# Expert 1's rows turned by TensorE from copies instead of through memory, and a new order around the late tiles

## The chip, the cores and the metric

The kernel runs on one core of a Trainium2 chip. Its time is the device time of one execution in microseconds (us); lower is better. TensorE (PE in the profile) multiplies, VectorE (DVE), ScalarE (ACT) and GpSimd (POOL) do the elementwise work, and SyncE (SP) issues most of the DMAs.

## The reference

Retention over 8 batches, 8 heads, 576 positions and head dimension 64, and then a mixture of experts on its output (4608 tokens of width 512, 8 experts of hidden width 1024):

```python
scores = (q @ k.T) / 8                       # per batch and head
ret = scores * gamma[h] ** (i - j)           # where j <= i, else 0
x = (ret @ v), heads side by side            # 4608 x 512
do = x @ w_skip > 0                          # tokens below stay as they are
e = argmax(x[do] @ w_gate); g = softmax(x[do] @ w_gate)[e]
y = g * (relu(x[do] @ w1[e]) @ w2[e])        # one expert for each token
out = x;  out[do] += y
```

## The kernel before, in words

**Retention.** The 4608 tokens are 36 tiles of 128; a batch is 4.5 tiles, so two batches make nine tiles, and `place(g)` is a tile's number among them. Each tile loads `q_t[g]` (queries and keys, turned) and `v_t[g]` (values, and keys as rows for the running state), 512 KB each, by `load` on SyncE's queue; six tiles of the first and four of the second are in flight. TensorE forms scores, state, values and the part carried from the state; VectorE applies masks and decays (`causal`, `decayed`); GpSimd scales the values (`scale`). `stage_c` turns the tile back, and it is written to `out`. The state ends with the tile whose place is 8: `state` returns there at once.

**Routing.** Logits come by four tiles. `GROUPS` are runs of tiles after which `route` picks each token's expert, its gate and its rank among its expert's tokens. It is a generator, and `spare` lets it run in VectorE's spare time of each tile. Its `gates` ends in five small operations by `pool` on GpSimd, which write the gate in three parts and the products `mc`. `slot_match` and `slot_add` then give the slots of tokens as a matrix product into `ps_m`. After the second group the most frequent expert so far is chosen to be expert 0 (`choose_first`), and its weights are loaded while retention still runs: chunk f at tick `LOADED[f]`, its high half cast on ScalarE two ticks later, its low half made on GpSimd in pieces by `lower`. After the fourth group (`KCUT`, tiles 24 to 27) `close_first` fetches the first 256 rows of expert 0, and GpSimd copies them by chunk (`by_chunk`) for `turn_early` on TensorE.

**Experts.** Weights come in 64 chunks (expert, eighth of the hidden width) of 512 KB into four raw tiles (`RAW`) and are split in a high and a low half (`split_w`: ScalarE the high, VectorE the low); each product is three matmuls. Expert 0 has up to 368 rows, in three blocks. The two early blocks run through chunks 0 to 5 as soon as they are there: `up_early`, `rectify`, `down_early`. The third block, `late`, is fetched by `late_ids` when all tiles are routed, turned by `turn_first`, and runs through these chunks by `up_late` and `down` in `experts`, six steps with the product of step f behind the up of step f + 1. In a late step ScalarE copies `part` out of PSUM, and VectorE makes `part`, `hhil` and `hlol` of it (lines 544 to 548). From chunk 6 on all three blocks run together, and then the other experts, one chunk after the other; `between` holds work to be done at places (expert, chunk, 0 before the down or 1 behind it).

**The next expert's rows** are gathered by indirect DMAs (`gather_next`), stored to memory (`stow`), read back by quarters of their columns (`spread`), turned in 32x32 blocks on VectorE (`turn_quarters`) and split in halves (`split_turned`). For expert 1 the store is issued on SyncE ahead of the weights of expert 1, the read at the end of step 5.

**Small work around it.** `expert_ids` writes the order of the experts, of which SyncE loads registers for the addresses of weights. `slot_rest` makes the target rows and gates that `finish` needs, `rank_caps` the room of each expert, which only `count_more` reads at the end.

**What sets the order.** TensorE's instructions stand in the order written. So do all that `vec`, `pool` and `keep` issue, on their engines. ScalarE's copies and casts are free: a scheduler places them by its own estimate of when they are ready. Each engine then runs its queue in order.

Of the kernel before, what the change touches and what calls it, by code (L numbers as in the profile page):

```python
# [23 lines left out]
P = 128  # L24
# [6 lines left out]
Q = 32  # L31
# [20 lines left out]
RAW = 4  # L52
GROUPS = (8, 8, 8, 4, 8)
KONE = 1
LOADED = (0, 3, 6, 8, 10, 12)
KCUT = 3
LAST = len(GROUPS) - 1
CUT = 2 * P
# [7 lines left out]
def kernel(  # L66
# [132 lines left out]
    def route(ps, k, post):  # L199

        t0, n = starts[k], GROUPS[k]
        nb = [P, n, NE]
        l8 = lg[:, t0 : t0 + n, 0:NE]
        mx = rt.tile([P, n], F32, tag="mx", name=f"mx_{t0}")
        vec("tensor_reduce", mx, l8, axis=AX.X, op=ALU.max)
        yield 210
        ls = rt.tile(nb, F32, tag="ls", name=f"ls_{t0}")
        vec("tensor_tensor", ls, l8, mx.unsqueeze(2).broadcast_to(nb), ALU.subtract)
        yield 210
        ex = rt.tile(nb, F32, tag="ex", name=f"ex_{t0}")  # L210
        nc.scalar.activation(ex, ls, AF.Exp)
        oh = rt.tile(nb, F32, tag="oh", name=f"oh_{t0}")
        vec("scalar_tensor_tensor", oh, ls, 0.0, desc.unsqueeze(1).broadcast_to(nb), ALU.is_equal, ALU.mult)
        yield 210
        m2 = rt.tile([P, n], F32, tag="m2", name=f"m2_{t0}")
        vec("tensor_reduce", m2, oh, axis=AX.X, op=ALU.max)
        yield 210
        vec("tensor_tensor", oh, oh, m2.unsqueeze(2).broadcast_to(nb), ALU.is_equal)
        yield 210
        mb = mks[:, t0 : t0 + n, :]  # L220
        skip = lg[:, t0 : t0 + n, NE : NE + 1].broadcast_to(nb)
        vec("scalar_tensor_tensor", mb, skip, 0.0, oh, ALU.is_gt, ALU.mult)
        yield 210
        at = flushed[0]
        pe.append(lambda: ranks(ps, k, mb))
        if k < LAST:
            yield from total(k, mb)
            if k == KONE:
                pe.append(lambda: count(ps, cum[:, k + 1, :], CNT))
        yield from gates(t0, n, ex, mb)  # L230
        while flushed[0] == at:
            yield WAIT
        mk = rt.tile(nb, F32, tag="mk", name=f"mk_{t0}")
        c0 = NE * NCMP * NBLK + t0 * NE
        vec("tensor_tensor", mk, ps[:, c0 : c0 + n * NE].rearrange("p (t e) -> p t e", e=NE), mb, ALU.mult)
        yield 210
        vec("tensor_reduce", trank[:, t0 : t0 + n], mk, axis=AX.X, op=ALU.add)
        yield 210
        if k == KONE:
            yield from choose_first(ps)  # L240
        for t in range(t0, t0 + n):
            while len(rs_t) == NR:
                yield WAIT
            slot_match(t)
            adds.append(lambda t=t: slot_add(ps, t, False, t == NT - 1))
            yield 260
        if post:
            at = flushed[0]
            pe.append(lambda: count(ps, cum[:, k + 1, :], CNT + NE))
            while flushed[0] == at:  # L250
                yield WAIT
            yield from post()
# [25 lines left out]
        vec("tensor_tensor", cum[:, k + 1, :], cum[:, k, :], some, ALU.add)  # L278
        yield 200

    def gates(t0, n, ex, mb):
        sm = rt.tile([P, n], F32, tag="sm", name=f"sm_{t0}")
        vec("tensor_reduce", sm, ex, axis=AX.X, op=ALU.add)
        yield 210
        vec("tensor_scalar", sm, sm, 1e-9, None, ALU.add)
        yield 200
        gt = rt.tile([P, n], F32, tag="gt", name=f"gt_{t0}")
        vec("reciprocal", gt, sm)
        yield 200
        cp = comps[:, t0 : t0 + n, :]  # L290
        pool("tensor_copy", cp[:, :, 2], gt)
        pool("tensor_tensor", gt, gt, cp[:, :, 2], ALU.subtract)
        pool("tensor_copy", cp[:, :, 3], gt)
        pool("tensor_tensor", cp[:, :, 4], gt, cp[:, :, 3], ALU.subtract)
        pool(
            "tensor_tensor",
            mc[:, t0 : t0 + n, :].rearrange("p t (e k) -> p t e k", k=NCMP),
            mb.unsqueeze(3).broadcast_to([P, n, NE, NCMP]),
            cp.unsqueeze(2).broadcast_to([P, n, NE, NCMP]),
            ALU.mult,  # L300
        )
# [252 lines left out]
    with ExitStack() as actx:  # L554
# [8 lines left out]

        q_t, v_t = {}, {}

        def behind(ins, other):
            tc.add_manual_dep(
                ins.ins,
# [4 lines left out]

        def load(into, n, g):
            into[g] = ap.tile([P, 2, DM], F32, tag="qv"[n], name=f"{'qv'[n]}_{g}", bufs=(QBUFS, VBUFS)[n])
            nc.sync.dma_start(into[g].rearrange("p s i -> p (s i)"), qkv[g, n])

        load(q_t, 0, 0)
        nc.scalar.dma_start(tt_sb, ttab)
# [41 lines left out]

        def head(a, r):
            return 2 * a + (r ^ (a & 1))

        def place(g):
            return g % NPD

        def scores(g):

# [442 lines left out]
    def spread(e):  # L1072

        n = span(e)
        xq[e] = mp.tile([P, -(-CAPS[1] // Q), P], F32, tag="xq", name=f"xq_{e}", bufs=1)
        for q in range(NQD):
            rows = xr[e][:, q * P : (q + 1) * P].rearrange("(g a) f -> a g f", a=Q)
            keep(nc.sync.dma_start(xq[e][q * Q : (q + 1) * Q, : n // Q, :], rows))

    def turn_quarters(e, c):  # L1080

# [13 lines left out]
    def experts():  # L1095
# [20 lines left out]
        def at(e, f, place, do, *args):  # L1116
            between.setdefault((e, f, place), []).append(lambda: do(*args))

        def turn_next(e):
            xT[e] = [mp.tile([P, NCC, CAP], F32R, tag=x, name=f"{x}_{e}") for x in ("xhi", "xlo")]  # L1120
            if e > 1:
                at(e - 1, 0, 1, lambda: stow(e, xg[e]))
                at(e - 1, 2, 0, spread, e)
            places = [(4, 0), (5, 0), (5, 1), (6, 0), (7, 0)] if e > 1 else [(6, 0), (6, 1), (7, 0), (7, 1), (7, 1)]
            for c, where in enumerate(places):
                if c:
                    at(e - 1, *where, split_turned, e, *xT[e], c - 1)
                if c < NCC:
# [1 line left out]

        at(NE - 1, 4, 1, count_more)
        for e in range(2, NE):
            at(e - 2, 4, 1, lambda e=e: gather_next(e, xg))

        load_raw(NFC - 1)
        gather_next(1, xg)
        by_chunk(*late[0], nc.scalar.copy)
        down_early(4)
        turn_first(late, range(NCC), "pt")
        down_early(5)  # L1140
        expert_ids()
        regs[1:] = expert_regs()[1:]
        split_raw(1)
        slot_rest(idf)
        rank_caps()
        stow(1, xg[1])
        py[0].append(bank("py2", "py_0_2"))
        turn_next(1)
        at(0, NCUT - 1, 1, spread, 1)
        for cur in steps + [None]:  # L1150
            if cur:
                e, f, ks = cur
# [29 lines left out]
            for do in between.pop((*place, 1), ()) if place else ():  # L1182
                do()
            if cur:
                split_raw(sum(chunks.index(c) < i + AHEAD for c in raw))
                load_raw(len(chunks))
            last = cur
        assert not between

    py = {0: [bank(f"py{c}", f"py_0_{c}") for c in range(CUT // P)]}  # L1190

    def down_early(f):
        down(0, f, early, py[0], hs[0, f], wq[0, f])

    for f in range(2, NCUT):
        hs[0, f] = hidden(mp, f)
    down_early(0)
    rectify(phs[2], early, hs[0, 2])
    rectify(phs[3], early, hs[0, 3])
    flush()  # L1200
    late_ids(ps_m)
    rectify(phs[4], early, hs[0, 4])
    down_early(1)
# [5 lines left out]
    count(ps_m, cum[:, LAST + 1, :], CNT + 2 * NE)  # L1209
    up_early(5)  # L1210
    rank_experts(ps_m)
    rectify(phs[5], early, hs[0, 5])
    idf = slot_ids(ps_m)
    down_early(3)

    experts()
    mctx.__exit__(None, None, None)
# [107 lines left out]
```

## Time and profile before

| | |
|---|---|
| Median of 3 runs | 424.06 us (421.91 to 425.01) |
| The profiled execution | 422.39 us |
| Its span, first to last instruction | 420.5 us |
| Mean granted TensorE clock | 0.966 |
| TensorE busy | 391.8 us (93%) |
| VectorE, ScalarE, GpSimd busy | 261.3, 151.1, 126.3 us |
| Bytes moved | 100.99 MB |

Busy shares are means over stages that are limited by different things. The granted clock is a share of full speed. A row of a timeline is an instruction, or several alike that follow each other (x4): its start, its time, and in brackets the idle time of the engine ahead of it with what ended that. A matmul's time is modelled and overlaps the next; from start to start is what counts.

### The profile page before, as it was taken

What the parts mean: (1) busy time and instruction counts of PE and PEld (TensorE: products, weight loads), DVE (VectorE), ACT (ScalarE), POOL (GpSimd) and SP (SyncE); (2) the same over time, 40 slices, a digit from 0 to 9 for tenths busy, and PEclk for the clock granted to TensorE, in tenths of its full rate; (3) what the DMA queues carried; (4) which work ended last, traced back from release to release, by engine and by line L of the source; (5) the groups of instructions that cost most, each with busy time, mean ns of one, the idle gap of its engine ahead of it and who ended that gap; (6) DMA issues with size and microseconds to landing.
All of it is one profiled execution on the core that took longest, in us unless ns stands there. A gap on an engine that the chain in (4) does not pass through costs nothing. (4 is left out here: it accounts for less than half of the span.)

```text
span 420.5 us, 11764 instructions
## 1 busy us (share of the span) xinstructions
PE 391.8 (93%) x4828; PEld 352.1 (84%) x4828; DVE 261.3 (62%) x567; ACT 151.1 (36%) x264; POOL 126.3 (30%) x169
## 2 busy tenths in 40 slices
PE   8989999998998999779799999999999999999970
PEld 4768878777777888668499999999999999999970
DVE  3655775774587647624755665766667567667740
ACT  1222322322333451134334534535535435554110
POOL 5422241233364842400052033042042222402102
PEclk9999999999999999967799999999999999999996
DMA  8999999999998631378298569577886678854001
GB/s 311 408 395 324 375 338 325 377 303 409 385 398 275 227 145 48 77 280 218 72 286 251 143 213 280 187 214 249 256 247 226 189 247 269 241 189 146 29 2 54
DMA packets 40456, 100.99 MB, mean 240 GB/s; under 512 B 4619, under 2 KB 13579, under 8 KB 40400
## 3 DMA queue, kind: packets, MB, share of 16 engines
q1 hardware_dynamic: 31440, 80.62, 57.5%
q0 software_dynamic: 3488, 10.03, 7.2%
q10 hardware_dynamic: 5472, 9.56, 6.0%
q8 instruction: 39, 0.64, 0.6%
q14 instruction: 17, 0.14, 0.1%
HBM read 81.49 MB, written 19.07 MB: 239 GB/s over the span
## 5 line engine op out<-in xcount | busy, mean ns | idle before, releaser
L164 ACT CAST whi_w<-w 128x1024 fp32r<-128x1024 f32 x58 | 60.9, 1050 | 53.2 <-PE py L503 33.7
L1043 POOL DMA_INDIRECT out<-rs,sidx x24 | 35.0, 1457 | 149.8 <-DVE rs L1039 148.9
L503 PE MATMUL ph<-xhi,whi_w 128*128 128x344 f32 (+6 forms) x224 | 69.7, 311 | 1.5 <-ACT xhi L171 1.4
L165 DVE TENSOR_TENSOR wlo_w<-w,whi_w 128x1024 fp32r<-128x1024 f32 x58 | 69.9, 1205 | 0.0
L503 PE MATMUL ph<-xlo,whi_w 128*128 128x344 f32 (+6 forms) x224 | 68.7, 306 | 1.1 <-DVE xlo L172 1.0
L503 PE MATMUL py<-hlo,whi_w 128*128 128x344 f32 (+6 forms) x224 | 67.9, 303 | 1.7 <-DVE hlo L527 1.6
L503 PE MATMUL py<-hhi,whi_w 128*128 128x344 f32 (+6 forms) x224 | 68.2, 305 | 0.0
L503 PE MATMUL ph<-xhi,wlo_w 128*128 128x344 f32 (+6 forms) x224 | 68.2, 304 | 0.0
L503 PE MATMUL py<-hhi,wlo_w 128*128 128x344 f32 (+6 forms) x224 | 67.7, 302 | 0.0
L670 POOL TENSOR_TENSOR v<-v,tt_sb 128x512 f32<-128x512 f32 x36 | 37.6, 1044 | 80.3 <-DVE xt L177 61.3
L527 DVE SCALAR_TENSOR_TENSOR hlo<-ph,hhi 128x344 fp32r<-128x344 f32 (+7 forms) x58 | 27.4, 474 | 46.3 <-ACT hhi L526 46.0
L177 DVE TENSOR_TENSOR sc<-psc,mask 128x512 f32<-128x512 f32 x72 | 46.3, 684 | 11.4 <-PE psc L635 6.4
L760 ACT COPY xn<-px 128x512 f32<-128x512 f32 x36 | 21.1, 587 | 84.1 <-PE px L758 74.0
L177 DVE TENSOR_TENSOR xt<-pxt,gt_sb 128x256 f32<-128x256 f32 x72 | 27.1, 418 | 38.2 <-PE pxt L728 35.5
L526 ACT ACTIVATE hhi<-ph 128x344 fp32r<-128x344 f32 (+7 forms) x58 | 24.7, 425 | 67.6 <-PE ph L503 67.5
L503 PEld LDWEIGHTS ph<-xhi,whi_w 128*128 128x128 f32 x224 | 42.4, 189 | 3.2 <-ACT xhi L171 3.1
L503 PEld LDWEIGHTS ph<-xlo,whi_w 128*128 128x128 f32 x224 | 42.5, 190 | 2.2 <-DVE xlo L172 2.1
L503 PEld LDWEIGHTS py<-hlo,whi_w 128*128 128x128 f32 x224 | 42.2, 188 | 2.1 <-DVE hlo L527 2.1
L503 PEld LDWEIGHTS ph<-xhi,wlo_w 128*128 128x128 f32 x224 | 42.6, 190 | 0.0
L503 PEld LDWEIGHTS py<-hhi,wlo_w 128*128 128x128 f32 x224 | 42.2, 188 | 0.0
L503 PEld LDWEIGHTS py<-hhi,whi_w 128*128 128x128 f32 x224 | 42.2, 188 | 0.0
L707 PE MATMUL pxt<-sc,v 128*64 128x128 f32 x576 | 40.0, 275 | 0.3 <-DVE sc L177 0.2
(185 smaller groups left out, 608.1 us busy)
## 6 DMA issues: line engine op xcount, KB each, us to landing
w<-w SPq DMA_DIRECT2D x64, 512.0 KB, 4.4
q<-qkv SPq DMA_DIRECT2D x36, 512.0 KB, 6.9
v<-qkv SPq DMA_DIRECT2D x36, 512.0 KB, 6.1
out<-xn ACTq DMA_DIRECT2D x36, 256.0 KB, 5.2
xr<-xg SPq DMA_DIRECT2D x7, 512.0 KB, 4.9
xq<-xr SPq DMA_DIRECT2D x12, 144.0 KB, 6.1
xq<-xr SPq DMA_DIRECT2D x8, 176.0 KB, 6.3
xq<-xr SPq DMA_DIRECT2D x8, 160.0 KB, 5.8
```

The costliest lines, as they stand in the source:

```text
L164: nc.scalar.copy(hi, t)
L165: ins = nc.vector.tensor_tensor(lo, t, hi.bitcast(F32), ALU.subtract)
L177: ins = getattr(nc.vector, name)(*args, **kw)
L503: nc.tensor.matmul(ps, x, y, start=first and n == 0, stop=last and n == 3 * len(terms) - 1)
L526: nc.scalar.activation(hi, ph, AF.Relu)
L527: keep(nc.vector.scalar_tensor_tensor(lo, ph, 0.0, hi.bitcast(F32), ALU.max, ALU.subtract))
L670: ins = nc.gpsimd.tensor_tensor(v, v, vt_sb[:, place(g), :].unsqueeze(2).broadcast_to([P, H, D]), ALU.mult)
L707: nc.tensor.matmul(pxt[a % 2][halves[j], a // 2, :], v[:, head(a, r), :], sc[:, r, a, :], start=a < 2, stop=t == 0 and a >= NPR - 2, skip_ ...
L760: nc.scalar.copy(xn, px)
L1043: put = nc.gpsimd.indirect_dma_start(out=out, out_offset=bass.IndirectOffsetOnAxis(ap=sidx[:n, k, e : e + 1], axis=0), in_=rs[:n], in_offs ...
```

## The change

- Expert 1's gathered rows are copied by chunk on GpSimd (`copy_rows`) and turned by TensorE (`turn_rows`: three transposes for each of four chunks, at steps 6 and 7 of expert 0). `stow` and `spread` remain for experts 2 to 7. Expert 2's gather is issued two steps later.
- `slot_rest` and `rank_caps` go to the ends of steps 5 and 6, chunk 6's split to the end of step 1; in the late steps a chunk is split one step later.
- The early down of chunk 0 is done by blocks, with the slot adds between them; that of chunk 3 goes ahead of the late turn, that of chunk 5 between the first two late ups. `slot_ids` is issued ahead of the last early `rectify`.
- The gates of the fourth group go from GpSimd to VectorE.
- Tiles of place 8 load only the values' half of `v_t`.
- Chunks 3, 4 and 5 of expert 0 have later ticks.

```diff
-LOADED = (0, 3, 6, 8, 10, 12)
+LOADED = (0, 3, 6, 9, 12, 13)
...
-        yield from gates(t0, n, ex, mb)
+        yield from gates(t0, n, ex, mb, vec if k == KCUT else pool)
...
-        pool("tensor_copy", cp[:, :, 2], gt)
-        pool("tensor_tensor", gt, gt, cp[:, :, 2], ALU.subtract)
+        on("tensor_copy", cp[:, :, 2], gt)
+        on("tensor_tensor", gt, gt, cp[:, :, 2], ALU.subtract)
...
-            nc.sync.dma_start(into[g].rearrange("p s i -> p (s i)"), qkv[g, n])
+            width = 2 * DM if n == 0 or place(g) < NPD - 1 else DM
+            nc.sync.dma_start(into[g].rearrange("p s i -> p (s i)")[:, :width], qkv[g, n, :, :width])
...
+    def copy_rows(e, xg):
+
+        xq[e] = mp.tile([P, NBLK * NCC, P], F32, tag="xq", name=f"xq_{e}", bufs=1)
+        for k, n in blocks(e):
+            x = xg[:n, k, :].rearrange("p (q c b) -> p c q b", q=NQD, b=Q)
+            y = xq[e][:n, k * NCC : (k + 1) * NCC, :].rearrange("p c (q b) -> p c q b", b=Q)
+            keep(nc.gpsimd.tensor_copy(y, x))
...
+        def turn_rows(e, c):
+
+            pt = bank(("pt", "py3", "m")[c % 3], f"pt_{e}_{c}")[:, : CAPS[e]]
+            for k, n in blocks(e):
+                nc.tensor.transpose(pt[:, k * P : k * P + n], xq[e][:n, k * NCC + c, :], ident[:n, :n])
+            split(*(x[:, c, : CAPS[e]] for x in xT[e]), pt)
...
-            at(e - 2, 4, 1, lambda e=e: gather_next(e, xg))
+            at(e - 2, 4 if e > 2 else NCUT, 1, lambda e=e: gather_next(e, xg))
...
         by_chunk(*late[0], nc.scalar.copy)
+        down_early(3)
+        turn_first(late, range(NCC), "pt")
         down_early(4)
-        turn_first(late, range(NCC), "pt")
-        down_early(5)
         expert_ids()
         regs[1:] = expert_regs()[1:]
-        split_raw(1)
-        slot_rest(idf)
-        rank_caps()
-        stow(1, xg[1])
         py[0].append(bank("py2", "py_0_2"))
-        turn_next(1)
-        at(0, NCUT - 1, 1, spread, 1)
+        copy_rows(1, xg[1])
+        for c, where in enumerate(((6, 0), (6, 1), (7, 0), (7, 0))):
+            at(0, *where, turn_rows, 1, c)
+        at(0, 0, 0, down_early, NCUT - 1)
+        at(0, 1, 1, split_raw, 1)
+        at(0, NCUT - 1, 1, slot_rest, idf)
+        at(0, NCUT, 1, rank_caps)
...
-                split_raw(sum(chunks.index(c) < i + AHEAD for c in raw))
+                split_raw(sum(chunks.index(c) < i + AHEAD - (i < NCUT) for c in raw))
...
-    down_early(0)
+    down_early(0, early[:1])
     rectify(phs[2], early, hs[0, 2])
     rectify(phs[3], early, hs[0, 3])
     flush()
+    down_early(0, early[1:])
...
+    idf = slot_ids(ps_m)
     rectify(phs[5], early, hs[0, 5])
-    idf = slot_ids(ps_m)
-    down_early(3)
```

## Rows read from the trace of the kernel before

**Rows 1.** Stretches: length, busy time (instructions) of each engine, clock, DMA share, GB/s.

```profile
core 0: us, PE busy (x) PEld busy (x) DVE busy (x) ACT busy (x) POOL busy (x), PEclk, DMA share, GB/s
30.00:130.00 100.00, 95.68 (x2172) 78.63 (x2170) 65.31 (x175) 29.77 (x60) 35.49 (x47) 1.00 0.98 359
150.00:175.20 25.20, 24.97 (x215) 20.92 (x211) 16.37 (x56) 7.86 (x18) 8.72 (x15) 1.00 0.22 73
175.20:188.00 12.80, 7.86 (x33) 6.90 (x33) 4.06 (x18) 3.24 (x6) 3.66 (x4) 0.69 0.82 272
188.00:200.00 12.00, 11.99 (x50) 10.39 (x50) 5.81 (x12) 5.02 (x8) 0.00 (x0) 0.76 0.73 193
200.00:211.30 11.30, 8.65 (x23) 5.63 (x23) 8.46 (x14) 3.34 (x6) 0.98 (x1) 0.70 0.33 87
222.00:400.00 178.00, 177.85 (x1291) 177.01 (x1290) 119.64 (x200) 81.80 (x134) 42.33 (x33) 1.00 0.68 210
```

**Rows 2.** Timeline of TensorE: start, time, line, operands, idle time before and its end.

```profile
177.26 0.77 PE L503 MATMUL py<-whi_w,hhil 128*112 128x512 f32 x1 [2.13 <-DVE hhil L547]
...
188.01 0.77 PE L503 MATMUL py<-whi_w,hhil 128*112 128x512 f32 x1 [2.89 <-DVE hhil L547]
...
200.97 0.42 PE L503 MATMUL ph<-xhi,whi_w 128*128 128x344 f32 x1 [0.95 <-ACT xhi L171]
```

**Rows 3.** Timeline of VectorE.

```profile
173.58 1.26 DVE L165 TENSOR_TENSOR wlo_w<-w,whi_w 128x1024 fp32r<-128x1024 f32 x1
174.77 0.16 DVE L177 TENSOR_SCALAR far<-idf 128x24 f32<-128x24 f32 x1
...
176.62 0.26 DVE L546 TENSOR_TENSOR part<-ph,part 128x112 f32<-128x112 f32 x1
...
199.85 0.55 DVE L1084 STREAM_TRANSPOSE xt<-xq 128x352 f32<-128x352 f32 x1 [3.54 <-DMA xq<-xr]
```

**Rows 4.** Timeline of ScalarE.

```profile
186.20 1.04 ACT L164 CAST whi_w<-w 128x1024 fp32r<-128x1024 f32 x1 [5.44 <-DMA w<-w]
187.15 0.24 ACT L544 COPY part<-ph 128x112 f32<-128x112 f32 x1
```

**Rows 5.** Timeline of SyncE's queue: issues of DMAs.

```profile
177.21 0.40 SPq L1068 DMA_DIRECT2D xr<-xg  x1
...
180.10 11.66 SPq L155 DMA_DIRECT2D w<-w  x5
192.28 1.87 SPq L1078 DMA_DIRECT2D xq<-xr  x4
```

**Rows 6.** Timeline of TensorE: first matmuls of products at full clock.

```profile
168.50 0.39 PE L503 MATMUL py<-whi_w,hhi 128*128 128x512 f32 x1
...
169.91 0.40 PE L503 MATMUL py<-whi_w,hhi 128*128 128x512 f32 x1
...
173.13 0.37 PE L539 MATMUL ph<-x,whi_w 128*128 128x224 f32 x1
...
174.07 0.33 PE L539 MATMUL ph<-x,whi_w 128*128 128x224 f32 x1
...
195.06 0.39 PE L503 MATMUL py<-whi_w,hhil 128*112 128x512 f32 x1
...
195.75 0.50 PE L503 MATMUL ph<-x,whi_w 128*128 128x368 f32 x2
...
197.77 0.40 PE L503 MATMUL py<-whi_w,hhi 128*128 128x512 f32 x1
```

**Rows 7.** Timeline of TensorE: a tile's transposes, then the early turn.

```profile
148.18 0.66 PE L758 MATMUL px<-ident,xt 128*128 128x128 f32 x4
148.67 1.16 PE L797 MATMUL pt_early<-ident,xp 128*128 128x128 f32 x8
```

**Rows 8.** Timeline of GpSimd: the last of the five gate operations, the copies by chunk.

```profile
136.72 0.46 POOL L183 TENSOR_TENSOR mc<-mks,comps 128x160 bf16<-128x160 bf16 x1
...
147.63 1.16 POOL L408 COPY xp<-xg 128x512 f32<-128x512 f32 x2
```

**Rows 9.** Waits, whole run and 0 to 30 us: total, times, longest.

```profile
POOL v L670 <- DMA v<-qkv: 11.1, 5, 2.9
```

More of the change, by code (lines that the diff above doesn't have):

```diff
@@ L279, in total, with gates @@
         yield 200
-    def gates(t0, n, ex, mb):
+    def gates(t0, n, ex, mb, on):
         sm = rt.tile([P, n], F32, tag="sm", name=f"sm_{t0}")
@@ L290, in gates @@
         cp = comps[:, t0 : t0 + n, :]
-        pool("tensor_copy", cp[:, :, 2], gt)
-        pool("tensor_tensor", gt, gt, cp[:, :, 2], ALU.subtract)
-        pool("tensor_copy", cp[:, :, 3], gt)
-        pool("tensor_tensor", cp[:, :, 4], gt, cp[:, :, 3], ALU.subtract)
-        pool(
+        on("tensor_copy", cp[:, :, 2], gt)
+        on("tensor_tensor", gt, gt, cp[:, :, 2], ALU.subtract)
+        on("tensor_copy", cp[:, :, 3], gt)
+        on("tensor_tensor", cp[:, :, 4], gt, cp[:, :, 3], ALU.subtract)
+        on(
             "tensor_tensor",
@@ L564, with place @@
         q_t, v_t = {}, {}
+        def place(g):
+            return g % NPD
         def behind(ins, other):
@@ L623, in head @@
             return 2 * a + (r ^ (a & 1))
-        def place(g):
-            return g % NPD
         def scores(g):
@@ L1074, in spread @@
         n = span(e)
-        xq[e] = mp.tile([P, -(-CAPS[1] // Q), P], F32, tag="xq", name=f"xq_{e}", bufs=1)
+        xq[e] = mp.tile([P, NBLK * NCC, P], F32, tag="xq", name=f"xq_{e}", bufs=1)
         for q in range(NQD):
@@ L1078, in spread @@
             keep(nc.sync.dma_start(xq[e][q * Q : (q + 1) * Q, : n // Q, :], rows))
+    def copy_rows(e, xg):
+        xq[e] = mp.tile([P, NBLK * NCC, P], F32, tag="xq", name=f"xq_{e}", bufs=1)
+        for k, n in blocks(e):
+            x = xg[:n, k, :].rearrange("p (q c b) -> p c q b", q=NQD, b=Q)
+            y = xq[e][:n, k * NCC : (k + 1) * NCC, :].rearrange("p c (q b) -> p c q b", b=Q)
+            keep(nc.gpsimd.tensor_copy(y, x))
     def turn_quarters(e, c):
@@ L1117, in at, with both @@
             between.setdefault((e, f, place), []).append(lambda: do(*args))
-        def turn_next(e):
[L1120 to L1125, printed above, removed]
+        def both(e):
+            return [mp.tile([P, NCC, CAP], F32R, tag=x, name=f"{x}_{e}") for x in ("xhi", "xlo")]
+        xT[1] = both(1)
+        def turn_rows(e, c):
[3 more added lines that the diff above has]
+            split(*(x[:, c, : CAPS[e]] for x in xT[e]), pt)
+        def turn_next(e):
+            xT[e] = both(e)
+            at(e - 1, 0, 1, lambda: stow(e, xg[e]))
+            at(e - 1, 2, 0, spread, e)
+            for c, where in enumerate([(4, 0), (5, 0), (5, 1), (6, 0), (7, 0)]):
                 if c:
@@ L1190, with down_early @@
     py = {0: [bank(f"py{c}", f"py_0_{c}") for c in range(CUT // P)]}
-    def down_early(f):
-        down(0, f, early, py[0], hs[0, f], wq[0, f])
+    def down_early(f, ks=early):
+        down(0, f, ks, py[0], hs[0, f], wq[0, f])
     for f in range(2, NCUT):
         hs[0, f] = hidden(mp, f)
-    down_early(0)
+    down_early(0, early[:1])
     rectify(phs[2], early, hs[0, 2])
```

## The prediction

> **What bounds the kernel now.** I read the busy time of each engine by stage first [rows 1]. From 30 to 130 us, while retention runs over its 36 tiles, TensorE is busy 95.7 of 100 us at full clock and the DMA engines 0.98 of the time. From 150 to 175.2 TensorE has no gap to speak of, and from 222 to 400 it is busy 177.85 of 178 us. Between them lies one bad stretch: 175.2 to 211.3. TensorE is busy there for 7.86 + 11.99 + 8.65 = 28.5 of 36.1 us, and the granted clock is 0.69, 0.76 and 0.70; between the two levels, 2.4 and 1.2 GHz, that is 7.9 + 5.8 + 6.8 = 20.5 us at the lower one. Everything behind it follows at TensorE's pace, so what is won here is won at the end.
>
> Next, what TensorE's idle time there ends on [rows 2]: twice on `hhil`, the late block's hidden rows (2.13 and 2.89 us), then on `xhi`, expert 1's turned rows. Their causes stand on other engines. The first stall: VectorE makes the eight small operations of slot_rest and rank_caps from 174.77, and the first `part` only at 176.62 [rows 3]. The second: ScalarE's in-order queue holds a weight cast 5.44 us for its load, with the next `part` behind it [rows 4]. That load is late because SyncE stood waiting for expert 1's gathered rows, put them into memory at 177.21, and only then asked for expert 1's weights, at 180.10 [rows 5]. The third: the read back from memory is issued at 192.28 [rows 5], and VectorE waits until 199.85 for it [rows 3]. The clock falls in each of the three windows in which such a gap lies.
>
> **What TensorE must do in that stretch, at full clock.** Start to start [rows 6]: an early down of two blocks 169.91 - 168.50 = 1.41 us, so 0.235 a matmul; a late up 174.07 - 173.13 = 0.94; a late down 195.75 - 195.06 = 0.69; an up of expert 0 in full 197.77 - 195.75 = 2.02; from these a down in full, nine matmuls, 2.11, and an up of expert 1, 344 columns instead of 368, 1.89. From 175.2 to 211.3 that is six late downs, four late ups, chunks 6 and 7 up and down, and the first up of expert 1: 4.14 + 3.76 + 4.04 + 4.22 + 1.89 = 18.05 us. The stretch takes 36.1, so idle time and clock together cost 18.05. That is the most that can be won.
>
> **The change, part by part.**
> 1. Expert 1's rows without memory. Gone are two stores and four loads on SyncE's queue, their wait for the gather, and four VectorE transposes (0.55 each [rows 3], off the path once their data is there). The weights of expert 1 can be asked for when their register is there, near 174.5 (VectorE makes the order of experts just ahead of the low half at 173.58 [rows 3]) instead of 180.10, and land near 180 with the 6.1 us that the first took (asked for at 180.10, its cast at 186.20). Added on TensorE: 12 transposes; four of a tile take 148.67 - 148.18 = 0.49 [rows 7], so 1.47 in all, straight on the path. Added on GpSimd: three copies at 1.16 / 2 = 0.58 [rows 8], 1.74 us. The first gathered rows are in SBUF at about 177.2 (the store waited for them [rows 5]), so the copies end near 180. TensorE wants the first later: chunk 3's down now ends the early work, 169.91 [rows 6] and 1.1 of point 4, so the late turn is at 171; two early downs, six late ups, five late downs and an up follow, 2.82 + 5.64 + 3.45 + 2.02, which makes 185. GpSimd's next work, expert 2's gather, is moved behind the copies and is stored a chunk into expert 1. So the copies cost nothing.
> 2. VectorE takes late tiles first. slot_rest and rank_caps move behind the last late up, and chunk 6's low half (1.26 [rows 3]) into step 1. The 2.13 us stall goes; the early down of chunk 5 (1.41) stands between the first late up and its down and covers the copy and three VectorE operations. What is late next: a period of a late step is 0.94 + 0.69 = 1.63 us on TensorE; its three VectorE operations, by the one at 176.62 some 0.28 each, take 0.85 and a low half 1.26, so in the two steps that hold one, 0.5 us can be short; and a ScalarE cast of 1.04 [rows 4] ahead of a `part` can delay it by as much. I put 1.5 us for the six steps (bounds 0, and 4.2, four casts in full; nearer to 0, since a cast can only hold what it is queued ahead of).
> 3. In steps 6 and 7 VectorE owes two low halves, chunk 6 and 7's hidden halves, four low halves of turned rows, slot_rest and rank_caps: by their rows about 10 us in 12. I put 0.7 us late at the first up of expert 1 (bounds 0 and 1.9, a whole up).
> 4. Gates of the fourth group on VectorE. Five operations leave GpSimd, of which the last takes 0.46 [rows 8], and go ahead of tile 31's slot matches and `xt`. On VectorE no row shows them; nearest are its small operations there: eight in 176.62 - 174.77 = 1.85 us, with smaller shapes for most, 0.23 each, so 1.2 us. GpSimd's release of that time helps nothing, since the fetch of the first rows waits for VectorE. Behind it everything to the chunk copies shifts; they begin at 147.63 and end at 148.79, and the early turn that reads them starts at 148.67 [rows 7, 8]. There is no slack, and TensorE is full from there on. Cost 1.1 us (bounds 0 and 1.5).
> 5. Closing tiles load values alone: 4 x 256 KB less. At 359 GB/s [rows 1] that is 2.9 us of transfer. VectorE and TensorE can gain it only if loads set the pace; all 11.1 us for which GpSimd waited for `v` fall in the first 30 us (the answer for them and the one for the whole run have the same row [rows 9]), ahead of the first closing tile. Value 0 (bounds 0, since less is moved, and 2.9).
> 6. Down of chunk 0 split round the slot adds, chunk 3's down moved ahead of the late turn, weights cast a few tiles later: the same TensorE work in another order; the late turn comes after as much work as its fetch needs. Nothing. If that cover fails, TensorE waits for the late rows, at most the early down that was moved, 1.41.
>
> Here two rules speak against the change. The Trainium skill, "VectorE: DVE Perf Modes", Rules for kernel authors, calls the VectorE transpose the fastest for 32x32 blocks. By operation the rows agree: the TensorE way costs 1.47 us of the bound engine and saves none of it; by the rule alone the sum would be 1.5 us slower, but it prices neither the store nor the load that fed that transpose. And "SBUF — State Buffer" says of the port pair of VectorE and GpSimd that it is held for a whole instruction, so the three copies could block VectorE operations with two SBUF inputs; by that the sum loses up to 1.7 us more, and no row here shows it.
>
> **The sum.** 18.05 - 1.47 - 1.5 - 0.7 - 1.1 = 13.3 us, if no gap is left that takes the clock down. The profiled execution took 422.39 us (span 420.5); the median of three was 424.06, 0.4% above. 422.39 - 13.3 = 409.1; by the median 410.8. Runs will scatter about the latter: 411.
>
> **Rivals.**
> - *One clock fall stays.* ScalarE's casts of expert 1's weights are not tied to the late steps; today one stands ahead of a `part` and waits 5.44 us for its load [rows 4]. Loads now come earlier, but so do the parts: a cast of a weight that lands at 180 to 184, ahead of a `part` due at 179 to 182, makes a gap of 2 to 3 us, and a block at the lower clock, where a third of 20.5 us loses up to 3.4. That gives back 5 to 6.5: 416 to 417.5. For it: the queue's present order; against: weight splits come a step later now.
> - *Loads set retention's pace too*: then 2.9 us more are won: 408. Against it: the waits for `v` end with the first 30 us.
> - *The other side: the ring of four weight tiles starves.* A new load waits for the low half of four chunks before; a load, a cast and a low half take 6.1 + 1.04 + 1.26 = 8.4 us. VectorE has some 17 us of work in the 20 before expert 1 (point 3 included). If it falls back by more than about 8 us there, each of expert 1's eight chunks (3.8 us) waits for its weights at the lower clock: up to 8 x 3.8 = 30 us lost against 13 to 17 won, so 428 to 435. It decides where the load of chunk 3 of expert 1 is issued less than 8.4 us ahead of its use; chunk 7's low half, which frees its tile, ends near 184, and its use is three steps behind the first up, near 204: 20 us.
> - *It doesn't do what it says*: TensorE waits for GpSimd's copies as it now waits for memory. They would have to end 13 us later than I count; then 424.
>
> **How the numbers follow.** Forecast as in the sum, 408 to 414.5: 0.53. One clock fall or as much in small stalls, 414.5 to 419.8: 0.22. Retention faster too, below 408: 0.08. Within 1% (4.2 us, about what a measurement tells apart): 0.10, from the copies' case and from several stalls together. Slower: 0.07, the starving ring. Faster by over 1% is 0.53 + 0.22 + 0.08 = 0.83. The range takes the forecast, most of the clock fall, and about half of the quicker case by its bounds: 406.5 to 418.
>
> **What would show it.** Right: granted clock 1.00 from 150 to 400; no store of expert 1's rows; expert 1's first weight load near 174.5; the first up of expert 1 near 193 (185, then the turns, a late down, an up, a down and the 1.5 of point 2) instead of 200.97; the early turn about 1 us later. Wrong: a TensorE wait of over 2 us on `hhil` or `xhi`, with clock below 0.8 in that window; a `v` wait gone from retention, with tiles closer together; weight loads issued under 8.4 us ahead of use.

## The result and the profile after

The changed kernel took 408.52 us (median of 4 runs, 408.13 to 410.65), the kernel before beside it 423.82 us: a ratio of 0.965, 95% interval 0.960 to 0.970. The prediction was 411.0 us, 406.5 to 418. The profiled execution took 408.29 us, span 406.6, against 422.39 and 420.5.

The stretches of the changed kernel, with the columns of [rows 1]:

```profile
core 0: us, PE busy (x) PEld busy (x) DVE busy (x) ACT busy (x) POOL busy (x), PEclk, DMA share, GB/s
150.00:175.20 25.20, 25.11 (x216) 21.11 (x217) 15.73 (x55) 9.50 (x18) 9.72 (x16) 1.00 0.26 84
175.20:188.00 12.80, 12.42 (x82) 11.01 (x81) 7.68 (x24) 5.07 (x10) 4.69 (x6) 1.00 0.70 238
188.00:200.00 12.00, 11.19 (x63) 9.81 (x63) 10.69 (x17) 7.04 (x12) 2.14 (x2) 1.00 0.60 175
200.00:211.30 11.30, 11.30 (x73) 11.30 (x73) 5.33 (x8) 4.45 (x6) 3.72 (x4) 1.00 1.08 293
```

From 175.2 to 211.3 TensorE is busy 34.9 of 36.1 us at full clock, where it was busy 28.5 at 0.69 to 0.76 [rows 1]. The clock stays at 1.00 until 398 us, where TensorE's work has ended. In its first two windows 1.19 us of idle time are left. 98.50 MB are moved instead of 100.99. What TensorE still waits for between 150 and 215 us (total, times, longest):

```profile
PE pt L1137 <- DVE xlo L172: 0.6, 1, 0.6
PE ph L503 <- DVE xlo L172: 0.3, 1, 0.3
PE py L503 <- DVE hhil L547: 0.2, 1, 0.2
PE pt_early L798 <- POOL xp L408: 0.2, 1, 0.2
```

The three stalls of [rows 2] are gone. TensorE's timeline shows the late steps, the turns of expert 1's rows and its first two ups:

```profile
179.22 0.22 PE L540 MATMUL ph<-x,wlo_w 128*128 128x112 f32 x1
179.67 0.49 PE L503 MATMUL py<-whi_w,hhil 128*112 128x512 f32 x1 [0.24 <-DVE hhil L547]
...
185.97 0.46 PE L1137 MATMUL pt<-ident,xq 128*128 128x128 f32 x3
186.22 0.46 PE L503 MATMUL py<-whi_w,hhil 128*112 128x512 f32 x1
...
189.34 0.46 PE L1137 MATMUL pt<-ident,xq 128*128 128x128 f32 x3
190.35 0.52 PE L1137 MATMUL pt<-ident,xq 128*128 128x128 f32 x3 [0.55 <-DVE xlo L172]
190.65 0.48 PE L503 MATMUL py<-whi_w,hhi 128*128 128x512 f32 x1
...
192.82 0.32 PE L503 MATMUL ph<-xhi,whi_w 128*128 128x344 f32 x1
...
194.34 0.42 PE L503 MATMUL ph<-xlo,whi_w 128*128 128x344 f32 x1 [0.26 <-DVE xlo L172]
...
197.32 0.32 PE L503 MATMUL ph<-xhi,whi_w 128*128 128x344 f32 x1
```

Expert 1's second up starts at 197.32 instead of 211.28 us: 13.96 earlier, and the span is 13.9 shorter. So the whole gain lies ahead of that instruction. Up to the routing of the fourth group the two executions took the same time: VectorE starts on that group's logits (its `lg`) at 130.18 and, before, at 130.15 us. The early turn starts at 149.44 instead of 148.67 [rows 7], so from there to the second up, the **turn** of the texts below, it is 47.88 us instead of 62.61.

SyncE's queue has no store and no read of expert 1's rows, and asks for its weights from 174.53 on instead of 180.10 [rows 5]. The row holds eight loads within 21.77 us; two are asked for at once, the others as tiles come free:

```profile
174.53 21.77 SPq L155 DMA_DIRECT2D w<-w  x8
```

ScalarE's casts still wait for loads, each with a `part` behind it, but for 1.6 to 1.8 us instead of 5.44 [rows 4]:

```profile
179.77 1.05 ACT L164 CAST whi_w<-w 128x1024 fp32r<-128x1024 f32 x1 [1.62 <-DMA w<-w]
180.72 0.24 ACT L544 COPY part<-ph 128x112 f32<-128x112 f32 x1
...
184.27 1.05 ACT L164 CAST whi_w<-w 128x1024 fp32r<-128x1024 f32 x1 [1.84 <-DMA w<-w]
185.22 0.24 ACT L544 COPY part<-ph 128x112 f32<-128x112 f32 x1
```

The gates of the fourth group on VectorE's timeline; their last operation ended on GpSimd at 137.18 before [rows 8]:

```profile
134.61 0.40 DVE L177 CAST comps<-gt 128x4 bf16<-128x4 f32 x1
135.04 0.64 DVE L177 TENSOR_TENSOR gt<-gt,comps 128x4 f32<-128x4 f32 x1
...
136.13 0.32 DVE L177 TENSOR_TENSOR mc<-mks,comps 128x160 bf16<-128x160 bf16 x1
```

The copies by chunk on GpSimd ended at 148.79 before [rows 8], and begin there now:

```profile
148.79 1.16 POOL L408 COPY xp<-xg 128x512 f32<-128x512 f32 x2
```

### The profile page after: what moved, and what is told of

Its sections match the earlier page's. It is cut to its first block, busy times and chain, and to the rows that moved or that the text cites. A ratio compares the mean times of both kernels' runs of the same rounds, so it can differ in the third digit from the quotient of the medians.

```text
span 406.6 us, 11777 instructions
## 1 busy us (share of the span) xinstructions
PE 382.8 (94%) x4840; PEld 346.4 (85%) x4840; DVE 260.3 (64%) x568; ACT 150.5 (37%) x264; POOL 126.5 (31%) x167
## 2 busy tenths in 40 slices
DMA packets 38600, 98.50 MB, mean 242 GB/s; under 512 B 4523, under 2 KB 12075, under 8 KB 38544
## 5 line engine op out<-in xcount | busy, mean ns | idle before, releaser
L164 ACT CAST whi_w<-w 128x1024 fp32r<-128x1024 f32 x58 | 60.9, 1051 | 47.9 <-DMA w<-w 25.1
L1044 POOL DMA_INDIRECT out<-rs,sidx x24 | 34.1, 1422 | 135.1 <-DVE rs L1040 134.1
L503 PE MATMUL ph<-xhi,whi_w 128*128 128x344 f32 (+6 forms) x224 | 68.8, 307 | 0.0
L503 PE MATMUL ph<-xlo,whi_w 128*128 128x344 f32 (+6 forms) x224 | 67.7, 302 | 0.3 <-DVE xlo L172 0.3
```

Of the source, the lines that this page charges most:

```text
L164: nc.scalar.copy(hi, t)
L503: nc.tensor.matmul(ps, x, y, start=first and n == 0, stop=last and n == 3 * len(terms) - 1)
L1044: put = nc.gpsimd.indirect_dma_start(out=out, out_offset=bass.IndirectOffsetOnAxis(ap=sidx[:n, k, e : e + 1], axis=0), in_=rs[:n], in_offs ...
```

## The experiments

Theory: the gain is two things that both stood on SyncE's queue, turned rows that came late through memory and weights queued behind their store, and the order around the late tiles only takes what is left of the stalls. Rivals: the order alone does it; the way through memory alone does it; the clock would stay up of itself. The kernels ran in three series, each beside the kernel before (medians 423.33, 424.69 and 423.88). A turn is read from one profiled execution, the clock in the three stretches from 175.2 to 211.3.

| kernel | us, median | ratio (95%) | turn, us | granted clock |
|---|---|---|---|---|
| before | 423.8 | 1 | 62.6 | 0.69, 0.76, 0.70 |
| after, first series | 407.46 | 0.962 (0.958 to 0.967) | 47.9 | 1, 1, 1 |
| rows alone | 411.15 | 0.971 (0.966 to 0.975) | 50.2 | 0.87, 1, 1 |
| order alone | 419.89 | 0.988 (0.983 to 0.994) | 61.6 | 0.78, 0.81, 0.70 |
| gates on GpSimd | 406.15 | 0.957 (0.953 to 0.962) | 48.5 | 1, 1, 1 |
| closing tiles in full | 410.13 | 0.965 (0.961 to 0.969) | 49.7 | 0.87, 0.99, 1 |
| rows alone, kept warm | 408.57 | 0.962 (0.958 to 0.965) | 50.4 | 1, 1, 1 |
| splits as before | 407.20 | 0.959 (0.954 to 0.964) | 47.0 | 1, 1, 1 |
| less work on GpSimd | 407.35 | 0.959 (0.955 to 0.963) | 47.3 | 1, 1, 1 |
| after, third series | 408.21 | 0.964 (0.960 to 0.968) | 47.9 | 1, 1, 1 |
| gates on GpSimd, again | 406.78 | 0.960 (0.956 to 0.963) | 48.8 | 1, 1, 1 |
| order, late store | 418.07 | 0.986 (0.982 to 0.990) | 57.9 | 0.87, 0.94, 0.61 |
| casts kept in order | 405.57 | 0.957 (0.952 to 0.961) | 46.4 | 1, 1, 1 |

**The kernel after once more**, for a reference in the first series.

> The changed kernel once more, as the reference of this series: 408.5 us (408.1 to 410.7 so far), 0.965 of the kernel before.

It gave 407.46 us and the turn to 0.04 us. The three turns of this kernel are 47.88, 47.92 and 47.94 us; what differs between executions lies ahead, since the early turn starts at 148.58 to 150.66 us.

**Rows alone.** `copy_rows` and `turn_rows`, and expert 2's gather two steps later; the order, the gates, the ticks and the loads as before.

```diff
-        stow(1, xg[1])
-        turn_next(1)
-        at(0, NCUT - 1, 1, spread, 1)
+        copy_rows(1, xg[1])
+        for c, where in enumerate(((6, 0), (6, 1), (7, 0), (7, 0))):
+            at(0, *where, turn_rows, 1, c)
```

> Only expert 1's rows by copies and TensorE turns (and expert 2's gather two steps later); the rest as before. Theory (the path through memory holds the weights and the turned rows, the order only the first stall): the second and third stall go with their clock falls, the first of 2.13 us stays with a block at the lower clock worth up to 3.4 us, and the 12 transposes cost 1.47: 18.05 - 2.1 - 3.4 - 1.5 = 11 us won, 413 us. Rival (the order of VectorE is what matters): under 5 us won, 419 us or more.

It took 411.15 us, 2 us less than the theory said (its block at the lower clock, below, was half as long as priced), and the turn is shorter by 12.4 of the 14.7 us. The first stall of [rows 2] is there, now 2.61 us, and the clock falls once behind it; in the window it is 0.87 of 12.8 us, so 3.3 us at the lower level. TensorE's row, and the window with the columns of [rows 1]:

```profile
179.66 0.49 PE L503 MATMUL py<-whi_w,hhil 128*112 128x512 f32 x1 [2.61 <-DVE hhil L547]
```

```profile
175.20:188.00 12.80, 10.19 (x61) 8.99 (x62) 9.01 (x28) 5.14 (x9) 6.89 (x8) 0.87 0.73 236
```

**Order alone.** The late tiles first, the split steps later, the early downs of chunks 3 and 5 moved; expert 1's rows through memory.

```diff
-        split_raw(1)
-        slot_rest(idf)
-        rank_caps()
         stow(1, xg[1])
+        at(0, 0, 0, down_early, NCUT - 1)
+        at(0, 1, 1, split_raw, 1)
+        at(0, NCUT - 1, 1, slot_rest, idf)
+        at(0, NCUT, 1, rank_caps)
```

> Only the order around the late tiles (slot_rest, rank_caps and the split of chunk 6 behind late steps, splits a step later, the early downs of chunks 3 and 5 moved); rows still through memory. Theory: the first stall of 2.13 us and its clock fall go, but the weights of expert 1 still wait for the store, so the late steps reach the casts that wait for their load sooner and stand there longer: 0 to 4 us won, 420 to 424 us, TensorE waits on hhil and xhi of together over 5 us. Rival (the order is what matters): 10 us won or more, 414 us or less.

419.89 us, at the theory's edge: 3.4 us less than the kernel before by the medians, and a turn 1.0 us shorter in the profiled execution. The order by itself gives little, since the cast still waits for a load that is asked for behind the store, and the stall only moves. TensorE's waits (total, times, longest), ScalarE's cast and SyncE's queue:

```profile
PE py L503 <- DVE hhil L547: 6.5, 2, 4.6
PE ph L503 <- DVE xlo L172: 2.2, 1, 2.2
```

```profile
184.78 1.04 ACT L164 CAST whi_w<-w 128x1024 fp32r<-128x1024 f32 x1 [5.15 <-DMA w<-w]
```

```profile
176.81 0.35 SPq L1070 DMA_DIRECT2D xr<-xg  x1
178.61 11.11 SPq L155 DMA_DIRECT2D w<-w  x4
189.88 1.87 SPq L1078 DMA_DIRECT2D xq<-xr  x4
```

**Order, late store.** To part the late weights from the late rows: the same, with the store behind the first two weight loads.

```diff
-        stow(1, xg[1])
+        at(0, 1, 0, lambda: stow(1, xg[1]))
```

> The changed order of the turn, with expert 1's rows still through memory, and the store of its rows put behind the first two weight loads of expert 1 instead of ahead of them (the kernel with the changed order alone had it ahead: waits of TensorE for a high half of 1.90 and 4.57 us at 180 and 187 us, and of 2.19 us for the turned rows at 202 us; ratio 0.988). Theory (two separate waits: weight loads that are queued behind a store, and turned rows that come late because they go through memory): the waits for a high half fall under 2 us together, the wait for the turned rows stays at 2 us or grows, with one fall of the clock there, and the ratio is 0.975 to 0.982. Rival A (the loads are late of themselves, not for the store): as with the order alone, 0.986 to 0.990. Rival B (the way through memory costs nothing once the loads are free): as the kernel after, 0.962 to 0.966.

The waits came out as the theory had them, the time did not: 0.986, just inside the first rival's figure, and not told apart from the order alone. The waits for a high half fall from 6.5 to 1.7 us and the turn by 3.7 us, but TensorE then waits 4.3 us for the turned rows instead of 3.4, and the clock of the last window falls to 0.61. TensorE's waits:

```profile
PE ph L503 <- ACT xhi L171: 3.1, 3, 1.3
PE py L503 <- DVE hhil L547: 1.7, 1, 1.7
PE ph L503 <- DVE xlo L172: 1.2, 1, 1.2
```

So with the way through memory kept, the new place of the store wins 3.7 us of the turn, and the turned rows still come late. That way is the larger part of the cost: the kernel after is 10 us shorter in the turn.

**Gates on GpSimd**, the kernel after with this one line back.

```diff
-        yield from gates(t0, n, ex, mb, vec if k == KCUT else pool)
+        yield from gates(t0, n, ex, mb, pool)
```

> The changed kernel with the fourth group's gates back on GpSimd. Theory (VectorE's five operations shift the copies by chunk, and the early turn with them): the early turn starts at 148.7 us instead of 149.4 with no wait for GpSimd, and 1.1 us are won: 407.4 us, 0.997 of the changed kernel. Rival (GpSimd's time is what the early turn waits for, so gates on VectorE help): the early turn later than 149.4 us, 409 us or more.

> The kernel after with the gates of expert 1 on GpSimd again, a second time. Theory (the gates on VectorE put the early turn off by 1.1 to 1.3 us): 0.955 to 0.960 of the kernel before and 1.0 to 1.6 us under the kernel after of the same series. Rival (the 1.3 us of the first time were chance): within 0.5 us of the kernel after.

406.15 and 406.78 us, 1.3 and 1.4 us below the kernel after of the same series: near the price. In the first series all six runs (404.18 to 406.64 us) lie below all six of the kernel after (407.10 to 409.13); in the third they overlap.

The delay itself can be read from the traces if it is counted from the fourth group's `lg`, just ahead of the gates. From there to the early turn it takes 19.25 to 19.29 us in the five traces with these gates on VectorE, and 18.15 to 18.94 in the nine with them on GpSimd; the medians are 1.0 us apart. VectorE's and TensorE's rows, the kernel after, then gates on GpSimd:

```profile
130.18 0.30 DVE L177 TENSOR_REDUCE lg<-pn 128x36 f32<-128x144 f32 x1
149.44 0.33 PE L798 MATMUL pt_early<-ident,xp 128*128 128x128 f32 x1 [0.53 <-POOL xp L408]
```

```profile
128.34 0.30 DVE L177 TENSOR_REDUCE lg<-pn 128x36 f32<-128x144 f32 x1
146.50 0.31 PE L798 MATMUL pt_early<-ident,xp 128*128 128x128 f32 x1
```

So the theory's mechanism is there, but not all of its rows. The early turn starts at 146.50 and 147.74 us and not at 148.7, since `lg`, which stands ahead of the edit, starts earlier too (128.34 and 129.59). And the turn is 0.6 and 0.9 us longer, behind waits for a high half of 0.94 and 1.44 us. By the traces, 1.1 us won ahead of the turn and these lost in it leave 0.5 and 0.3 us of the 1.3 and 1.4; where the rest lies stays open.

**Closing tiles in full**, the kernel after with all of `v_t` loaded.

```diff
-            width = 2 * DM if n == 0 or place(g) < NPD - 1 else DM
+            width = 2 * DM
```

> The changed kernel with the closing tiles' loads in full, 4 x 256 KB more. Theory (TensorE, not the loads, sets the pace of retention): no difference, 0.962 to 0.965 of the kernel before, as the changed kernel in its two series. Rival (loads set the pace): 2.9 us slower, 0.969 to 0.972.

410.13 us; the ratio is that of the kernel after in the first result, 0.965, and no kernel after ran in this series. The fourth group's `lg` starts at 130.02 us, where it starts at 129.29 to 131.41 in the kernel after: retention is no slower up to there. Its trace shows more than its time. The order of instructions on each engine is that of the kernel after, but the first cast of expert 1's weights starts at 181.17 instead of 179.77 us, and one `part` behind it makes TensorE wait 1.87 us instead of 0.24. The clock falls (a matmul of the next down goes from 0.40 to 0.63 us). ScalarE's timeline, then TensorE's:

```profile
181.17 1.04 ACT L164 CAST whi_w<-w 128x1024 fp32r<-128x1024 f32 x1 [3.24 <-PE ph L540]
182.12 0.25 ACT L544 COPY part<-ph 128x112 f32<-128x112 f32 x1
```

```profile
182.98 0.48 PE L503 MATMUL py<-whi_w,hhil 128*112 128x512 f32 x1 [1.87 <-DVE hhil L547]
183.30 0.40 PE L503 MATMUL py<-wlo_w,hhil 128*112 128x512 f32 x1
...
185.00 0.63 PE L503 MATMUL py<-wlo_w,hhil 128*112 128x512 f32 x1
```

The releaser named, a late up of TensorE, is only what ended last before it: in the kernel after the same cast starts 0.7 us ahead of that up (179.77 and 180.46). What was late is most likely the load itself, asked for at 174.36 here and at 174.53 there. This execution is probably no exception: of the six, four show a mean granted clock of 0.985 to 0.987 (409.93 to 410.65 us, this one among them) and two of 0.990 (408.59 and 409.08), while of the 16 executions of the kernel after two lie below 0.989. The mean doesn't say where a clock fell, so the fall in the turn is shown for this one alone. Whether smaller closing loads bring that load in earlier stays open.

**Rows alone, kept warm.** Rows alone, with twelve matmuls that feed nothing put into the 2.61 us stall.

```diff
+        at(0, 1, 0, keep_up, 12)
```

> The kernel with expert 1's rows by TensorE alone (411.2 us, 0.9705 of the kernel before), and twelve matmuls on constants, into a bank that nothing reads then, where TensorE waits 2.6 us for the first hhil. They add nothing to the result. Theory (the clock falls for the idle gap and costs its own share): granted clock 1.00 between 175 and 188 instead of 0.87, (1 - 0.87) x 12.8 = 1.7 us won, 0.966 to 0.967; the late step itself starts no earlier. Rival (the clock falls for the kind of work in the late steps, or the loss is the gap alone): clock as low as there, 0.970 or more.

408.57 us, 0.962 against 0.971 without them. The matmuls take the stall's place on TensorE, and the clock of the window stays at 1.00:

```profile
176.40 2.76 PE L103 MATMUL ps_m<-mc 128*128 128x512 bf16 x12
179.16 0.48 PE L503 MATMUL py<-whi_w,hhil 128*112 128x512 f32 x1
```

So the fall is caused by the gap, not by the kind of work behind it. The other executions fit: the mean granted clock is 0.979 to 0.987 in all six of rows alone and 0.988 to 0.992 in all seven of these. What the fall is worth isn't settled: the medians are 2.6 us apart, the theory said 1.7, and the two kernels ran in different series. The profiled execution was the slowest of its runs. In its turn the first up of expert 1 comes 1.2 us earlier than in rows alone, but TensorE then waits 1.2 us for the turned rows, so the turn is no shorter.

**Splits as before**, the kernel after without the later splits in the late steps.

```diff
-                split_raw(sum(chunks.index(c) < i + AHEAD - (i < NCUT) for c in raw))
+                split_raw(sum(chunks.index(c) < i + AHEAD for c in raw))
```

> The changed kernel with weights split as early in the late steps as before (one step earlier). Theory (casts that wait for loads stand ahead of part in ScalarE's queue): more waits on hhil, one of 1 to 3 us and perhaps a fall of the clock: 0.966 to 0.975 of the kernel before. Rival (the scheduler orders the casts by its own estimate, and the step in the program says little): same as the changed kernel, 0.962 to 0.965.

407.20 us; nothing is lost, and the only wait of TensorE left between 150 and 215 us is 0.2 us. The rival was right here: this edit does nothing for the gain.

**Less work on GpSimd** ahead of the copies by chunk: gates on GpSimd, one piece of a low half later, `rank_caps` and one split later. Of these edits the piece is shown.

```diff
-                lower(1 if g < NT - 6 else 2, first)
+                lower(1 if g < NT - 6 or g == NT - 3 else 2, first)
```

> A version built on the two series: the changed kernel, gates on GpSimd (0.957 of the kernel before), one piece of weights less on GpSimd ahead of the copies by chunk, one split later in step 6, rank_caps a step later. Theory (what TensorE still waits for is 0.4 us at the early turn and 0.8 us on xlo behind VectorE's low halves): 0.5 to 1.2 us below the version with gates alone, 0.954 to 0.956. Rival (VectorE's order only moves the waits): as with the gates alone, 0.957.

407.35 us, no better than the gates alone. TensorE's wait at the early turn is gone, and nothing comes of it.

**The kernel after, third series.**

> The kernel after once more, beside the other kernels of this series. Both theories: 0.962 to 0.966 of the kernel before, with 42.5 to 44 us from the start of the early turn to the first up of expert 1. A half-clock block between the two in this run would bear out that the load's landing alone decides on it: 3.4 us longer then.

408.21 us, with 43.45 us from the early turn to the first up of expert 1. No clock fall in the turn of this execution: in none of the three traces of this kernel did one occur there.

**Casts kept in order.** The casts of expert 1's weights are the last thing that a `part` can stand behind. Here they hold the place that the program gives them.

```diff
-        nc.scalar.copy(hi, t)
+        keep(nc.scalar.copy(hi, t))
...
-        nc.scalar.copy(part, ph[:, 0])
+        keep(nc.scalar.copy(part, ph[:, 0]))
```

> The kernel after with the gates of expert 1 on GpSimd again, and with ScalarE held to the program's own order for two of its operations: the casts of a weight tile to its high half and the copies of the late tiles' parts. Theory (the only thing left in the turn is a part that stands behind a cast which waits for its load: 1.6 and 1.8 us of waiting at the cast in the kernel after, and one fall of the clock of 3.41 us when the load landed later): no part stands behind a waiting cast, no wait of TensorE for a high half over 0.5 us between the early turn and the first up of expert 1, clock 1.00 there, 0.954 to 0.957 of the kernel before and not slower than the kernel with the gates alone. Rival (the casts then stand later than the weights are wanted, so that the first ups of expert 1, or the rounds before, wait for them): a wait of over 1 us on a high half at or behind the first up of expert 1, 0.960 or more.

405.57 us, the lowest median of all, 0.957 of the kernel before. The theory's rows are there: no `part` behind a cast that waits, 0.3 us of waiting, and a turn of 46.4 us, 2.4 less than with the gates alone. With the gates alone TensorE waited 0.94 and 1.44 us for a high half. (In this execution the clock did fall once in retention, behind a wait of TensorE of 1.79 us at 103 us.) ScalarE's timeline, then TensorE's waits:

```profile
179.41 0.25 ACT L544 COPY part<-ph 128x112 f32<-128x112 f32 x1 [1.42 <-PE ph L540]
181.52 0.25 ACT L544 COPY part<-ph 128x112 f32<-128x112 f32 x1 [1.85 <-PE ph L540]
181.67 1.05 ACT L164 CAST whi_w<-w 128x1024 fp32r<-128x1024 f32 x1
```

```profile
PE py L503 <- DVE hhil L547: 0.3, 1, 0.3
PE pt_early L798 <- POOL xp L408: 0.2, 1, 0.2
```

Against the kernel after of its series the ratio of medians is 405.57 / 408.21 = 0.9935. Against the gates alone the intervals overlap, so of the 2.4 us that the traces show 1.2 appear in the medians, and that isn't more than the runs scatter.

## Why the prediction was right

The mechanism and its order of size held: the stretch's idle time and lower clock were what could be won, 18.05 us, and the terms against it came to 4.8 us by the sum and come to 3.9 by the traces. That these are so near is in part luck: three terms were too large, by 0.4, 0.6 and 0.3 us, and one too small by 0.5. The signs named beforehand are there: the first weight load at 174.53, the first up of expert 1 at 192.82 against 193, the early turn 0.8 us later, and the granted clock 1.00.

- **Point 1, transposes**, 1.47 us. Three of them take 0.25 us from start to start (185.97 to 186.22), 0.30 behind a wait (190.35 to 190.65), so about 1.05 in all. The price was taken from a tile's four transposes, which were 0.12 each; these are 0.08. The copies ended well ahead of their use, as counted, and the weight loads begin at 174.53, as counted. The rule of the Trainium skill, "VectorE: DVE Perf Modes", Rules for kernel authors, that I held against the change was not the one that bears on it: it is about blocks of 32x32, and the row above it in the same table names TensorE for a transpose of 128x128. Nor did the rows agree with it by operation, as I wrote: VectorE's four transposes took 0.54 to 0.55 us each, 2.2 in all, TensorE's twelve 1.05. What holds is that these 1.05 us stand on the bound engine and VectorE's didn't, and rows alone still took 12.4 us off the turn.
- **Point 2, late steps**, 1.5 us. A down that follows its up directly starts 0.06 us behind the last matmul of the up (183.15 to 183.21 in this kernel). Three downs start 0.23, 0.45 and 0.36 us behind it (at 177.66, 179.67 and 181.59), so 1.04 - 3 x 0.06 = 0.86 us were lost; the 0.24 of the waits is only a part. For two of them the reason is the one given: ahead of 179.67 VectorE's operations stand behind a low half, ahead of 181.59 a `part` stands behind a cast. Ahead of 177.66 neither does: ScalarE's copy of `part` starts at 176.79, and the profile names TensorE's own down as what it waited for. The bound of 4.2 was never near, but closing tiles in full shows 1.87 us at one step alone.
- **Point 3, the first up of expert 1**, 0.7 us. `xlo` is late twice: the fourth turn starts 190.35 instead of 189.59 (0.25 behind the third), and in the last quarter of the up its second matmul 0.42 late (193.76 + 0.16 to 194.34). That is 1.2 us: the term was too small by 0.5, within its bounds of 0 and 1.9. VectorE's backlog of 10 us in 12 was real: from the up of chunk 6 on, 183.95 to 195.95, it is busy 10.16 us.
- **Point 4, gates**, 1.1 us. The five operations take 1.77 us from 134.61 to 136.38 instead of the 1.2 I took: the first two, 0.40 and 0.64 us, are longer than any of the eight from which I took the price, and end when GpSimd's pieces of a low half beside them end (below). The copies begin 1.16 us later and the early turn 0.77, in two executions in which `lg` starts 0.03 us apart. Against the same kernel with the gates back on GpSimd the early turn comes 1.1 us later, counted from `lg`.
- **Point 5, closing tiles**, 0. All of GpSimd's waits for loads of `v` are still in the first 30 us (8.9 us now, 11.1 before [rows 9]), so loads don't set the pace of retention. Whether the smaller loads matter later, in the turn, is open (above).
- **Point 6**, nothing: right for the splits (splits as before), and the early downs cover what they were to cover: TensorE shows no wait at the late turn (170.86). The later ticks of chunks 3 to 5 did not run by themselves.

By these terms 18.05 - 1.05 - 0.86 - 1.18 - 0.77 = 14.2 us, against 13.9 of the span and 13.3 predicted. Against the 409.1 of the sum the profiled execution is 0.8 us lower, out of the 2.5 by which the median lies under 411.0. The rest is the step from the profiled execution to the median: I added 1.7 us because the one before lay that far under its median, while the one after lies 0.2 under its own.

**The rivals.** One clock fall staying was the right one to fear: it is not in any of the kernel after's three traces, but rows alone and closing tiles in full have it, from waits of 2.61 and 1.87 us, at 411.15 and 410.13 us instead of the 416 to 417.5 that I gave it; I had taken the block at the lower clock as long as those of before, a third of 20.5 us, and added the gap in full. It was 3.3 and 3.6 us long, half of that, and what a late step waits is taken off later waits: the turn of closing tiles in full has none for `xlo` and is 1.8 us longer than the kernel after's, not 5. Loads setting the pace: no row for it. The ring of four tiles did not starve: TensorE waits for no weight behind the first up, and the clock is 1.00 there. That TensorE would wait for the copies did not happen.

The other rule cited from the Trainium skill, "SBUF — State Buffer", SBUF: two separate sides, on the port pair of VectorE and GpSimd that is held for a whole instruction, fits the traces, at another place than I looked for it. The first two gate operations on VectorE run beside two pieces of a low half on GpSimd, whose rows follow, and end 0.04 and 0.02 us behind them (135.01 and 135.68, the pieces at 134.97 and 135.66). The first of them takes 0.40 us; the third, of the same shape with no GpSimd operation beside it, 0.18. It is so in all five traces with these gates on VectorE, 0.40 and 0.64 us each time. A score's mask (`sc<-psc,mask`), which reads PSUM, isn't held up: it takes 0.68 us with or without GpSimd at work beside it. No run parts VectorE from GpSimd here, so that the port is the reason is argued from these times.

```profile
134.24 0.73 POOL L819 TENSOR_TENSOR wlo_w<-w,whi_w 128x256 fp32r<-128x256 f32 x1
134.94 0.72 POOL L819 TENSOR_TENSOR wlo_w<-w,whi_w 128x256 fp32r<-128x256 f32 x1
```

The copies of expert 1's rows do it too. In the kernel after's third series an `hhil` of a late step starts beside the last of them and takes 0.59 us instead of the 0.22 of one that runs alone:

```profile
180.38 0.60 POOL L1087 COPY xq<-xg 88x512 f32<-88x512 f32 x1 [0.81 <-DMA xg<-out,gidx]
180.46 0.59 DVE L547 TENSOR_SCALAR hhil<-part 128x112 fp32r<-128x112 f32 x1
```

That is 0.4 us at most, far from the 1.7 that I gave the rule: in the profiled kernel after the same `hhil` takes 0.35 us, and of VectorE's low halves only the one from 177.84 to 179.06 meets a copy, for 0.12 us, and took its usual 1.22 us.

## What to carry to other kernels

Add up, over the stretch in which the bound engine is interrupted, its idle time and what the lower clock costs; then ask of each stall which queue its cause stands in, since here the rows through memory and the weights behind their store were one queue, and an order that cures one stall alone gives 1.0 us of the turn's 14.7. Before a small operation is moved to VectorE, look what GpSimd does beside it: here two of five took two to four times as long as those behind them. Where an engine with a free scheduler holds small operations of the critical path, pin the large ones that can wait for a load behind them: that took the waits away here, though the medians don't settle what it is worth. Put a stall's chance next to when its load lands: the same order of instructions was free of falls in three executions of one kernel and had one where a cast stood 1.4 us later.

## What the runs showed that I had not expected

- A wait of TensorE of 1.87 us was followed by a fall from full clock, and one of 1.44 us (gates on GpSimd, again) was not. The length alone doesn't decide: a wait of 1.77 to 1.79 us in retention, at 103 to 106 us, was followed by a fall in two traces (casts kept in order; order, late store) and by none in two others (the third series of the kernel after; splits as before). Filling a wait of 2.61 us with matmuls that feed nothing kept the clock at 1.00.
- The first two of five dependent small operations on VectorE took 0.40 and 0.64 us for 4 columns, until GpSimd's pieces beside them had ended; the others took 0.17 to 0.32 us.
- The start of the early turn scatters by 4.3 us between single executions (146.50 to 150.84 us over all the kernels that ran), while the turn of the kernel after repeats to 0.06 us: changes of one or two us ahead of it can't be read from one trace. Counted from a row just ahead of the edit (`lg` above), the same traces tell 1.0 us apart.
